# The last product of a group of eight, issued as two halves of 256 columns

## The chip, the cores and the metric

One Trainium2 chip, of which the kernel uses one core. The metric is the device time of one execution in microseconds (us), and the kernel before has a median of 450.82 us over 3 runs.

## What is computed

Sliding-window attention with 32 global positions for 8 batches of 8 heads, then a mixture of 8 experts (hidden size 1024) on the 4352 rows of 512 values that the attention gives. A row takes part only where its skip score is positive, goes to one expert, and is replaced by itself plus the gated result.

```python
def _moe_ref(x, w_skip, w_gate, w1, w2):
    do_compute = x @ w_skip > 0
    out = x.copy()
    xc = x[do_compute]
    e_idx = np.argmax(xc @ w_gate, axis=1)      # gate_w: softmax of the logits at e_idx
    for e in range(E):
        mask = e_idx == e
        h = np.maximum(xc[mask] @ w1[e], 0.0)
        y[mask] = gate_w[mask, None] * (h @ w2[e])
    out[do_compute] = xc + y
    return out
```

## The kernel before

The first half of the program (to about 219 us) is the attention, with the routing of its rows to lists by expert. The change is in the second half, the expert stage. There the rows of an expert are gathered in tiles of 128, two tiles (256 rows) at a time. Weights and activations are split in a high and a low part, so that each product of fp32 accuracy is three matmuls: high by high, high by low, low by high. The eight experts run one after the other, and the weights, tokens and hidden tiles lie in two sets of buffers that alternate by expert.

`ffn` is the body of an expert. Line 933 makes the hidden values of both tiles: eight groups of 12 matmuls (128x256 each), one group for each 128 hidden units, every group into one of the four PSUM banks `sb`; ScalarE (line 939) and VectorE (line 940) turn each into the high and low parts `hh` and `hlw`. Then comes the first tile of results (`py0`, by `part(py0, 0, ...)`): eight product groups `f`, three matmuls of 512 columns each (line 950), and `put`, which scales by the gate, adds the row on VectorE (line 1047) and scatters it to the output from GpSimd (line 1051).

What follows depends on how many rows the expert has, read from a register at run time:

- few rows: `short`, a second tile of at most 64 rows, in two column halves of 256, two matmuls for each of eight groups (line 985), with its own VectorE operations (line 991);
- more rows: `full`, the whole second tile by `part(py, 1, ...)`, also at line 950. In the main body its last two product groups are held back and issued by `rest_of`, and its `put` (into `ylast`) comes at the end of the expert;
- over 256 rows: also a third tile, by `ffn_half` (the half body): hidden values with the operands the other way round (line 1012), transposes (line 1023), then eight product groups into `sb[3]` (line 1038) and `put`;
- still more rows: `beyond`, another `ffn` over the further rows of the list.

The order on each engine is the one in which the program is written (a manual schedule). In the program's order, line 933 of the next expert follows at once on TensorE behind the last matmul of line 985, of line 1038, or of `rest_of`. Transposes of the next expert's rows (line 211) are issued between the first and the second tile.

In the profiled execution, the main body of the experts 0 to 7 starts on TensorE at about 219, 265, 286, 307, 343, 364, 399 and 422 us. Expert 0 has a further list, whose line 933 starts at 243.76 us.

## Time and profile before

| | us |
|---|---|
| median of 3 runs | 450.82 (449.47 to 453.19) |
| the profiled execution, its own time | 450.12 |
| its span, first to last instruction | 448.2 |
| TensorE busy | 424.5 (95%) |
| TensorE weight loads busy (beside its matmuls) | 366.2 (82%) |
| VectorE, ScalarE, GpSimd busy | 308.3, 286.5, 223.3 |
| mean granted clock of TensorE | 0.992 of full speed |

The profile is of one execution. Times are counted from the first instruction; a row names the line, the engine, the operation, the tile written and the tiles read. PE is TensorE's matmul, PEld its weight load, DVE VectorE, ACT ScalarE, POOL GpSimd; a q behind an engine is its sequencer. Matmuls are pipelined: the start of one to the start of the next is what one costs, and its own duration is longer than that.

### The profile page before, as it was taken

What the parts mean: (1) busy time and instruction counts of PE and PEld (TensorE: products, weight loads), DVE (VectorE), ACT (ScalarE), POOL (GpSimd) and SP (SyncE); (2) the same over time, 40 slices, a digit from 0 to 9 for tenths busy, and PEclk for the clock granted to TensorE, in tenths of its full rate; (3) what the DMA queues carried; (4) which work ended last, traced back from release to release, by engine and by line L of the source; (5) the groups of instructions that cost most, each with busy time, mean ns of one, the idle gap of its engine ahead of it and who ended that gap; (6) DMA issues with size and microseconds to landing.
All of it is one profiled execution on the core that took longest, in us unless ns stands there. A gap on an engine that the chain in (4) does not pass through costs nothing.

```text
span 448.2 us, 13744 instructions
## 1 busy us (share of the span) xinstructions
PE 424.5 (95%) x5002; PEld 366.2 (82%) x5002; DVE 308.3 (69%) x1222; ACT 286.5 (64%) x872; POOL 223.3 (50%) x233
## 2 busy tenths in 40 slices
PE   7799999998989999978999999999999999999995
PEld 3587787877767877666997999999888999889894
DVE  6898787997878878986662249586724868249352
ACT  5599999999888998866451238375523745237240
POOL 7568677778985688887367114223101321013101
PEclk9699999999999999999999999999999999999999
DMA  7998999898999789531435607594910949209101
GB/s 255 314 317 271 312 322 315 278 326 279 287 261 322 231 239 288 161 120 49 81 134 118 247 31 271 193 316 161 346 74 9 314 181 353 106 22 319 72 4 34
DMA packets 50773, 93.35 MB, mean 208 GB/s; under 512 B 15820, under 2 KB 20172, under 8 KB 50672
## 3 DMA queue, kind: packets, MB, share of 16 engines
q1 hardware_dynamic: 44992, 79.73, 54.8%
q0 software_dynamic: 5680, 12.34, 8.7%
q8 instruction: 55, 0.90, 0.8%
q14 instruction: 46, 0.38, 0.3%
HBM read 81.07 MB, written 14.01 MB: 212 GB/s over the span
## 4 chain that ended last, share of the span: by engine, by line
DMA 43%; PE 19%; ACT 11%; issue 10%; DVE 8%; POOL 7%; SPq 1%; POOLq 1%; another core or an unknown queue 0%; ACTq 0%
DMA out_dram<-yo,six 18%; DMA xsecond<-out_dram,six 9%; ACT prob L403 8%; DMA xfirst<-out_dram,six 7%; DMA out_dram<-xr 4%; PE pv L544 4%; PE pss L385 3%; PE pst L481 3%; DVE prob L398 2%; DMA lst<-dat,slu 2%; POOL prob L440 2%; PE pr L602 2%; PE pv L556 1%; PE psg L449 1%; PE psgT L497 1%
## 5 line engine op out<-in xcount | busy, mean ns | idle before, releaser
L403 ACT ACTIVATE prob<-prob,nmx 128x160 f32<-128x160 f32 x256 | 106.8, 423 | 16.1 <-DVE nmx L398 15.3
L440 POOL TENSOR_TENSOR prob<-prob,inv 128x640 f32<-128x640 f32 x64 | 80.6, 1260 | 33.0 <-DVE inv L436 19.0
L1051 POOL DMA_INDIRECT out_dram<-yo,six x12 | 12.1, 1012 | 111.9 <-DVE yo L1047 108.6
L939 ACT ACTIVATE hh<-ph 128x256 fp32r<-128x256 f32 x72 | 27.7, 384 | 54.9 <-PE ph L933 47.3
L385 PE MATMUL pss<-ks,qs 64*64 64x160 f32 x1024 | 52.0, 309 | 1.8 <-DVE nmx L398 1.1
L403 ACT ACTIVATION_READ_ACCUMULATOR prob<-prob,nmx 128x1 f32 x256 | 49.6, 194 | 0.0
L544 PEld LDWEIGHTS pv<-ptT,vw 128*64 128x64 f32 x1024 | 41.4, 139 | 9.2 <-issue 8.6
L544 PE MATMUL pv<-ptT,vw 128*64 128x64 f32 (+1 forms) x1024 | 46.3, 238 | 0.0
L933 PE MATMUL ph<-xl,w1h 128*128 128x256 f32 x288 | 45.1, 279 | 0.2 <-DVE yo L991 0.2
L933 PE MATMUL ph<-xh,w1h 128*128 128x256 f32 x288 | 45.2, 279 | 0.0
L933 PE MATMUL ph<-xh,w1l 128*128 128x256 f32 x288 | 44.9, 278 | 0.0
L385 PEld LDWEIGHTS pss<-ks,qs 64*64 64x64 f32 x1024 | 35.1, 135 | 9.3 <-issue 5.3
L940 DVE SCALAR_TENSOR_TENSOR hlw<-ph,hh 128x256 fp32r<-128x256 f32 x72 | 30.1, 418 | 17.8 <-ACT hh L939 17.4
L693 POOL DMA_INDIRECT lst<-dat,slu x34 | 34.0, 1000 | 14.4 <-DVE cni L1080 5.8
L950 PE MATMUL py<-w2h,hh 128*128 128x512 f32 x104 | 41.1, 396 | 0.0
L950 PE MATMUL py<-w2h,hlw 128*128 128x512 f32 x104 | 40.6, 391 | 0.0
L950 PE MATMUL py<-w2l,hh 128*128 128x512 f32 x104 | 40.6, 390 | 0.0
L481 PE MATMUL pst<-ident,prob 128*128 128x128 f32 x256 | 39.7, 281 | 0.0
L933 PEld LDWEIGHTS ph<-xh,w1h 128*128 128x128 f32 x288 | 38.8, 188 | 0.3
L933 PEld LDWEIGHTS ph<-xl,w1h 128*128 128x128 f32 x288 | 38.5, 189 | 0.4 <-DVE yo L991 0.4
L933 PEld LDWEIGHTS ph<-xh,w1l 128*128 128x128 f32 x288 | 38.4, 188 | 0.0
L194 DVE TENSOR_TENSOR w2l<-raw,w2h 128x1024 fp32r<-128x1024 f32 x28 | 34.1, 1217 | 3.9 <-ACT w2h L193 3.9
(193 smaller groups left out, 990.3 us busy)
## 6 DMA issues: line engine op xcount, KB each, us to landing
raw<-in_w_dram SPq DMA_DIRECT2D x56, 512.0 KB, 6.2
vw<-in_v_dram SPq DMA_DIRECT2D x32, 512.0 KB, 6.4
ks<-in_kT_dram SPq DMA_DIRECT2D x32, 400.0 KB, 5.4
out_dram<-xr SPq DMA_DIRECT2D x32, 256.0 KB, 5.3
qs<-in_qT_dram SPq DMA_DIRECT2D x31, 256.0 KB, 4.9
raw<-in_w_dram POOLq DMA_DIRECT2D x8, 512.0 KB, 7.2
vgs<-in_vgl_dram SPq DMA_DIRECT2D x32, 64.0 KB, 6.4
lst<-dat,slu POOLq DMA_INDIRECT x34, 5.0
```

What stands on the lines that cost most here:

```text
L194: eng.tensor_sub(lo, raw, hi.bitcast(F32))
L385: nc.tensor.matmul(banks[odd][head(h ^ odd), j * W:(j + 1) * W], q[head(h), w * QB:(w + 1) * QB], window(k[head(h)], w), start=True, stop= ...
L403: nc.scalar.activation(pt[:, i, :], pt[:, i, :], AF.Exp, bias=nmx[:, i:i + 1], scale=-1.0, accum_out=sums[:, i, 0:1],)
L440: nc.gpsimd.tensor_mul(pt[:, sl, :], pt[:, sl, :], inv[:, sl].unsqueeze(2).to_broadcast([P, 4, W]),)
L481: nc.tensor.transpose(pst[:, i * P:(i + 1) * P], pt[:, 4 * hf + i, 0:KW], ident)
L544: nc.tensor.matmul(pv[head(h), j * 96:j * 96 + n], vv[:, w, head(h)], ptT[:, w, h ^ odd, 0:n], start=False, stop=j == 3, skip_group_check= ...
L693: ins = nc.gpsimd.indirect_dma_start(out=lst, out_offset=bass.IndirectOffsetOnAxis(ap=slu[:, t:t + 1], axis=0), in_=dat[:, bs[j], t - 4 * ...
L933: nc.tensor.matmul(ph[:, 0:GRP], hl[a][:, c, f * P:(f + 1) * P], bb[:, c, :], start=i == 0, stop=i == 3 * NC - 1,)
L939: nc.scalar.activation(hh[:, f, :], ph[:, 0:GRP], AF.Relu)
L940: nc.vector.scalar_tensor_tensor(hlw[:, f, :], ph[:, 0:GRP], 0.0, hh[:, f, :].bitcast(F32), ALU.max, ALU.subtract,)
L950: nc.tensor.matmul(py, a[:, f, t * P:(t + 1) * P], hl[bb][:, f, :], start=f == 0 and i == 0, stop=f == NF - 1 and i == 2,)
L1051: ins = nc.gpsimd.indirect_dma_start(out=out, out_offset=bass.IndirectOffsetOnAxis(ap=sidx, axis=0), in_=yo, in_offset=None, bounds_check= ...
```

## The change

In the second tile (`t` = 1) of `part` and in `ffn_half`, the last of the eight product groups is issued as two column halves: all three terms for the columns 0 to 255, then all three for 256 to 511, six matmuls of 256 columns where there were three of 512. The flag that closes the accumulation stands on the last of the six. The first seven groups, the first tiles, and `short` stay as they are, as do the operations that read the result.

```diff
     LAST = 2
+    WHOLE = [slice(0, DM)]
+
+    def tail(f):
+        return WHOLE if f < NF - 1 else [slice(c, c + 256) for c in range(0, DM, 256)]
+
@@ in ffn @@
         def part(py, t, fs):
             for f in fs:
-                for i, (a, bb) in enumerate(terms):
-                    nc.tensor.matmul(
-                        py, a[:, f, t * P:(t + 1) * P], hl[bb][:, f, :],
-                        start=f == 0 and i == 0, stop=f == NF - 1 and i == 2,
-                    )
+                for cs in tail(f) if t else WHOLE:
+                    for i, (a, bb) in enumerate(terms):
+                        nc.tensor.matmul(
+                            py[:, cs], a[:, f, t * P:(t + 1) * P], hl[bb][:, f, cs],
+                            start=f == 0 and i == 0, stop=f == NF - 1 and i == 2 and cs.stop == DM,
+                        )
@@ in ffn_half @@
-            for i, (a, bb) in enumerate(((hh, "w2h"), (hh, "w2l"), (hlw, "w2h"))):
-                nc.tensor.matmul(
-                    py, a[:, f, 0:P], hl[bb][:, f, :],
-                    start=f == 0 and i == 0, stop=f == NF - 1 and i == 2,
-                )
+            for cs in tail(f):
+                for i, (a, bb) in enumerate(((hh, "w2h"), (hh, "w2l"), (hlw, "w2h"))):
+                    nc.tensor.matmul(
+                        py[:, cs], a[:, f, 0:P], hl[bb][:, f, cs],
+                        start=f == 0 and i == 0, stop=f == NF - 1 and i == 2 and cs.stop == DM,
+                    )
```

## Rows read from the trace of the kernel before

**Rows 1.** The page: span, and busy time of TensorE (us, share, instructions).

```profile
span 448.2 us, 13744 instructions
PE 424.5 (95%) x5002; PEld 366.2 (82%) x5002; DVE 308.3 (69%) x1222; ACT 286.5 (64%) x872; POOL 223.3 (50%) x233
```

**Rows 2.** Busy us by stretch: length, PE, PEld, DVE, ACT, POOL; clock, DMA share, GB/s.

```profile
226.00:442.90 216.90, 216.11 (x1468) 198.02 (x1466) 123.85 (x184) 96.58 (x157) 55.47 (x54) 1.00 0.49 167
442.90:448.20 5.30, 0.00 (x0) 0.00 (x0) 0.96 (x2) 0.00 (x0) 0.91 (x1) 0.95 0.08 18
```

**Rows 3.** Waits of TensorE from 228 us on: us in total, times, longest.

```profile
PE xt L211 <- DMA xmore<-out_dram,six: 0.6, 1, 0.6
PE ph L933 <- DVE yo L991: 0.2, 1, 0.2
```

**Rows 4.** Instructions of lines 950 and 1047: count; ns min/median/max; first and last start.

```profile
L950 PE MATMUL py<-w2h,hlw x104: 388/389/398, 231.4 to 438.7; 128*128 128x512 f32 x104
...
L1047 DVE SCALAR_TENSOR_TENSOR ylast<-py,lt,xfirst x2: 750/750/751, 266.1 to 422.3; 128x512 f32<-128x512 f32 x2
L1047 DVE SCALAR_TENSOR_TENSOR yo<-ph,lt,xmore x2: 751/752/752, 342.8 to 399.3; 128x512 f32<-128x512 f32 x2
L1047 DVE SCALAR_TENSOR_TENSOR ylast<-py,lt,xsecond x2: 743/743/743, 343.4 to 400.0; 128x512 f32<-128x512 f32 x2
```

**Rows 5.** Timeline of TensorE in expert 7 (start, us, what): line 950, then 985.

```profile
437.99 0.39 PE L950 MATMUL py<-w2h,hlw 128*128 128x512 f32 x1
...
438.67 0.39 PE L950 MATMUL py<-w2h,hlw 128*128 128x512 f32 x1
438.89 0.28 PE L985 MATMUL py<-w2h,hh 128*128 128x256 f32 x1
...
439.61 0.28 PE L985 MATMUL py<-w2h,hh 128*128 128x256 f32 x1
```

**Rows 6.** The same of line 933 alone: length, PE, PEld; clock, DMA share, GB/s.

```profile
243.76:254.65 10.89, 10.89 (x96) 10.85 (x95) 1.00 0.87 316
286.37:297.27 10.90, 10.90 (x96) 10.86 (x96) 1.00 0.52 157
307.43:318.33 10.90, 10.90 (x96) 10.87 (x96) 1.00 0.50 149
342.51:353.82 11.31, 11.30 (x96) 11.26 (x95) 1.00 0.54 175
363.97:374.87 10.90, 10.90 (x96) 10.86 (x96) 1.00 0.52 163
399.04:410.35 11.31, 11.31 (x96) 11.26 (x95) 1.00 0.59 196
422.15:433.46 11.31, 11.31 (x96) 11.26 (x95) 1.00 0.07 26
```

**Rows 7.** Timeline of TensorE: what stands ahead of line 933 in four bodies.

```profile
243.53 0.40 PE L950 MATMUL py<-w2h,hlw 128*128 128x512 f32 x1
...
286.25 0.28 PE L985 MATMUL py<-w2l,hh 128*128 128x256 f32 x1
...
342.29 0.39 PE L1038 MATMUL ph<-w2h,hlw 128*128 128x512 f32 x1
...
421.92 0.39 PE L950 MATMUL py<-w2h,hlw 128*128 128x512 f32 x1
```

**Rows 8.** Timeline of TensorE's weight loads: end of expert 6, start of expert 7.

```profile
421.70 0.19 PEld L950 LDWEIGHTS py<-w2h,hlw 128*128 128x128 f32 x1
421.93 0.65 PEld L933 LDWEIGHTS ph<-xh,w1h 128*128 128x128 f32 x4
```

**Rows 9.** Timeline: VectorE's operation behind the half body of expert 3.

```profile
342.78 0.75 DVE L1047 SCALAR_TENSOR_TENSOR yo<-ph,lt,xmore 128x512 f32<-128x512 f32 x1 [2.83 <-PE ph L1038]
```

**Rows 10.** Branches of TensorE's sequencer (ns min/median/max; first and last start), end of expert 6.

```profile
L1189 PEldq COMPARE_BRANCH  x2: 83/1496/2909, 417.5 to 418.1; - x2
L1204 PEldq COMPARE_BRANCH  x1: 187/187/187, 421.0 to 421.0; - x1
```

## Prediction

> **What bounds the kernel now.** I read the page first: TensorE is busy 424.5 of 448.2 us [rows 1]. That is an average, so I then asked for the two stretches that matter to an edit in the expert stage. From 226 to 442.9 us TensorE is busy 216.11 of 216.90 us at a granted clock of 1.00, and in the 5.3 us that remain it does nothing: two DVE operations and one scatter end the kernel [rows 2]. The waits of TensorE in that stage are one of 0.6 us for a gather and one of 0.2 us for a DVE result [rows 3]. So the reader is to see a stage in which every nanosecond that TensorE's stream of products grows or shrinks moves the end by the same amount, and in which no other engine has to be asked first. The chain of waits on the page gives 18% to the DMA out_dram<-yo; it is a long span between a scatter and something much later, and TensorE never stands still for it, so I set that view aside.

> **What runs of the changed lines.** Line 950 issues each of its three terms 104 times, that is 13 groups of eight [rows 4]. Nine are first tiles (eight experts and the one further list of expert 0), which the change leaves alone. Four are second tiles: their results are the four 128x512 `ylast` operations of line 1047, two from xfirst and two from xsecond [rows 4]. The two 128x512 operations `yo<-ph` belong to half bodies [rows 4]. So six products change, in experts 0, 3, 5 and 6 (second tiles) and 3 and 5 (half bodies). In each, three 128x512 matmuls become six 128x256 ones: 18 more matmuls and 18 more weight loads run, nothing else is issued, and no DMA, wait or buffer is added. The put still reads all 512 columns and so still waits for the very last matmul.

> **Step A, the products themselves.** Three 512-column matmuls take 0.68 us from start to start (437.99 to 438.67), and right behind them six 256-column ones over the same two operands, hh and w2, take 0.72 us (438.89 to 439.61) [rows 5]. Each product therefore grows by 0.04 us, six by 0.24 us. As a lower bound, the fast pace of line 933 below, 10.90/96 = 0.1135 us a matmul, gives 0.68 and a growth of nothing. I take 0.24, because line 985 has the same operands. [...]

> The 18 extra weight loads take 0.19 us each [rows 8], 3.4 us in all. They cost nothing beyond this pace, because a load starts right behind the start of the matmul ahead of it (the load at 421.93, the matmul at 421.92 [rows 7, 8]) and is done while that one streams. If that cover went, 3.4 us would be the bill.

> **Step B, what comes behind them.** This is where I expect the larger term. Line 933 is the same 96 matmuls of 128x256 in every expert, yet it takes two different times [rows 6]: 10.89 or 10.90 us in four of the stretches shown, and 11.31 us in three. TensorE is busy throughout in both, the clock is 1.00 in both, and DMA does not sort them (a share of 0.87 in a short one, 0.07 in a long one). Nor do the buffers, which alternate by expert: experts 2 (at 286.37) and 4 (at 342.51) use the same ones and differ, and so do experts 3 (at 307.43) and 7 (at 422.15). What sorts them is what TensorE ran just before. Ahead of the 10.90 ones at 286.37, 307.43 and 363.97 stand the 256-column products of line 985 (the row at 286.25 is one of them); ahead of the 11.31 ones at 342.51, 399.04 and 422.15 stands a long run of 512-column products, line 1038 or line 950 (the rows at 342.29 and 421.92) [rows 7]. The stretch at 243.76 follows 512-column products too and is short; but there only six of them (two product groups, the last at 243.53 [rows 7]) stand behind the wait of 0.6 us for the gather [rows 3], which I read as too few to settle. So TensorE's stream seems to carry a phase over from one group to the next: a settled run of 512 columns hands on the slow one, 256-column products hand on the fast one, and line 933 keeps what it is handed for all 96.

> The change puts six 256-column products at exactly the three places ahead of a slow stretch. If six are enough to hand on the fast phase, three stretches save 0.41 us each, 1.23 us. That six are enough is a choice: behind 512 columns, line 985 goes from 438.89 to 439.61 at an even 0.12 us [rows 5], which is the pace that it holds for its 32. Against it: line 933 itself runs 96 matmuls of 256 columns in the slow phase without leaving it, so 256 columns alone is not the cure; the operands of w2 and hh may be.

> In expert 0 the changed product is followed by the stretch at 243.76, which is fast already, and in experts 3 and 5 the changed second tile by line 1012; I put nothing there. If the first lost its fast phase it would cost 0.41 us.

> **Step C, waits.** The put of a half body starts 0.1 us after the last matmul's end, at 342.78, and takes 0.75 us [rows 9]. Its bank is wanted again by the fourth of the eight groups of line 933, about 342.51 + 3 x 1.41 = 346.7 us, so a put that comes 0.04 us later is hidden by 3 us of other products. The put of a second tile is queued behind other DVE work and is no one's releaser on TensorE. The tail after 442.9 us is the short body of expert 7 and is not touched.

> **The sum.** +0.24 - 1.23 = -0.99 us. Against the profiled execution, 450.12 us (span 448.2), that is 449.13; against the median of the three runs, 450.82, it is 449.83. The four times known of the kernel lie from 449.47 to 453.19, and the middle of 450.12 and 450.82 is 450.47; from there the forecast is 449.5 us. A measurement of this kernel can tell about 1% from no change, 4.5 us, so this is no change.

> **The rivals.** *The phase doesn't flip.* Then step A stands alone: 450.47 + 0.24 = 450.7 us. For it speaks that line 933 never leaves the slow phase by itself; against it, the three fast stretches behind line 985. Chance 0.30.

> *The jump out of the expert's branch is no longer covered*, and the kernel is slower. At the end of expert 6 TensorE's sequencer spends 2.91 us in one compare-and-branch of line 1189 from 418.1, then 0.19 us in that of line 1204 from 421.0 [rows 10], while the engine works through the products queued ahead of it; the first load of the next expert starts at 421.93 [rows 8]. The margin is 421.93 - 421.19 = 0.7 us. The change lengthens the code of every expert, and the sequencer has six more instructions to pass ahead of that jump. A second stay of 2.91 us in that chain would leave 2.2 us of standing TensorE. Once, with step A, that is 452.9 us; at the ends of experts 3, 5 and 6 all three, 450.47 + 0.24 + 6.6 = 457.3 us. It decides from the point at which the second branch ends after 421.93. Against it: the two other branches there take 0.08 and 0.19 us [rows 10], and six more instructions come with 0.04 us more of products. [...] Chance 0.06 for one such place, 0.02 for all three.

> *Something makes it faster by over 1%.* Nothing in the stage is large enough: all seven stretches at the fast pace are worth 1.23 us. Chance 0.02.

> **How the numbers follow.** Flip 0.60 (449.5), no flip 0.30 (450.7), one uncovered jump 0.06 (452.9, within 1%), three 0.02 (457.3, slower), faster 0.02. The first three are all no change; for a median of three times that spread as those of before did I move 0.01 more to faster and 0.02 to slower, which gives faster 0.03, the same 0.93, slower 0.04. The range has to hold the first two cases and the spread of the runs: downward 449.47 - 0.99 = 448.5 and a little, upward 450.82 + 0.24 = 451.1 and some of the way to 453.19: 448.3 to 452.0 us.

> **What the changed profile would show.** Step A: lines 950 and 1038 with 36 matmuls of 128x256 in the place of 18 of 128x512, and 0.68 to 0.72 us from the first of six to the first of what follows. Step B right: the stretches of line 933 in experts 4, 6 and 7 at 10.90 instead of 11.31 us, their matmuls 276 ns instead of 281. Step B wrong: they stay at 11.31. Step C: no new waits of TensorE from 226 us on, and the put of a half body still 0.1 us behind its last matmul. The slower rival would show as idle TensorE ahead of the first load of line 933 in experts 4, 6 or 7. The prediction is wrong if TensorE stands still anywhere in the stage where it does not now, or if other pieces of its stream (lines 1012 and 950 behind the changed products) change pace by more than 0.2 us.

## The result

The changed kernel takes 455.37 us (median of 17 runs, 453.3 to 457.7), the kernel before 450.92 us (17 runs, 449.47 to 453.19): a ratio of 1.0091, with an interval of 1.0073 to 1.0109. It is slower by 0.9%, some 4.4 us. The forecast was 449.5 us in a range of 448.3 to 452.0, so it was wrong.

The page after, where TensorE is busy 2.5 us longer in a span that is 6.3 us longer (in [rows 1] 424.5 of 448.2):

```profile
span 454.5 us, 13779 instructions
PE 427.0 (94%) x5020; PEld 367.8 (81%) x5020; DVE 308.6 (68%) x1222; ACT 286.1 (63%) x872; POOL 223.4 (49%) x233
```

The 18 more matmuls are there (5020 instead of 5002). What is new is idle time. The waits of TensorE from 222 us on, beside which [rows 3] has only the last two (us in total, times, longest):

```profile
PE py L991 <- issue: 2.3, 1, 2.3
PE xt L211 <- issue: 1.3, 1, 1.3
PE xt L211 <- DMA xmore<-out_dram,six: 0.8, 1, 0.8
PE ph L938 <- DVE yo L997: 0.2, 1, 0.2
```

"issue" is a wait for nothing that the profile shows: no engine and no transfer releases it. So the next question is what TensorE's sequencer did. Line 991 is 985 of before, 938 is 933, 956 is 950 and 1045 is 1038. First its branches in the kernel before, at the same two places, expert 4's branch into the short body and expert 5's branch ahead of its half body (ns min/median/max; first and last start in us):

```profile
L1204 PEldq COMPARE_BRANCH  x1: 446/446/446, 355.9 to 355.9; - x1
L1186 PEldq COMPARE_BRANCH  x1: 2422/2422/2422, 381.6 to 381.6; - x1
```

and the same two in the changed kernel:

```profile
L1211 PEldq COMPARE_BRANCH  x1: 3033/3033/3033, 357.3 to 357.3; - x1
L1193 PEldq COMPARE_BRANCH  x1: 4605/4605/4605, 386.8 to 386.8; - x1
```

One branch takes 2.6 us longer, the other 2.2. The two waits stand differently to them. Expert 5's branch is no longer covered by the products queued ahead: it ends at 391.40 us, and behind the last of these products TensorE stands still for 1.3 us, up to the transposes of line 211:

```profile
390.30 0.39 PE L956 MATMUL py<-w2h,hlw 128*128 128x512 f32 x1
391.96 0.63 PE L211 MATMUL xt<-ident,xmore 128*128 128x128 f32 x4 [1.27 <-issue]
```

Expert 4's branch is still covered: TensorE works through it and is idle for 0.09 us behind it. The stop of 2.3 us comes 3 us after its end, inside the short body, behind 15 of its 32 matmuls, where nothing branches:

```profile
359.99 0.39 PE L956 MATMUL py<-w2h,hlw 128*128 128x512 f32 x1
360.47 1.07 PE L211 MATMUL xt<-ident,xsecond 128*128 128x128 f32 x8
361.29 0.36 PE L991 MATMUL py<-w2h,hh 128*128 128x256 f32 x1
...
363.04 0.28 PE L991 MATMUL py<-w2h,hh 128*128 128x256 f32 x1
365.63 0.28 PE L991 MATMUL py<-w2l,hh 128*128 128x256 f32 x1 [2.31 <-issue]
```

And line 938, the same seven bodies as in [rows 6] (length, PE, PEld; clock, DMA share, GB/s):

```profile
244.71:255.60 10.89, 10.89 (x96) 10.86 (x96) 1.00 0.89 316
287.66:298.56 10.90, 10.90 (x96) 10.87 (x96) 1.00 0.49 158
308.73:319.63 10.90, 10.90 (x96) 10.86 (x96) 1.00 0.50 159
343.86:354.76 10.90, 10.90 (x96) 10.87 (x96) 1.00 0.53 175
368.52:380.09 11.57, 11.57 (x96) 11.53 (x96) 0.94 0.51 157
405.76:416.66 10.90, 10.90 (x96) 10.87 (x96) 1.00 0.55 170
428.75:439.75 11.00, 11.00 (x96) 10.96 (x96) 1.00 0.07 26
```

The three stretches of 11.31 us are at 10.90, 10.90 and 11.00: what the change was forecast to give, it gives. But expert 5's, at 10.90 before, has a granted clock of 0.94 and takes 11.57. The stretch around it:

```profile
361.29:366.55 5.26, 2.95 (x26) 2.86 (x25) 1.85 (x4) 0.92 (x2) 1.02 (x1) 1.00 0.49 190
366.55:369.96 3.41, 3.41 (x18) 3.41 (x17) 1.36 (x3) 0.00 (x0) 0.00 (x0) 0.50 0.02 5
```

TensorE stood still for 2.3 us up to 365.63; from 366.55 to 369.96 its granted clock was 0.50, though it was busy all of that time. So more than the stop is lost here: the half clock begins 0.92 us after it ended.

The account, by the starts of line 938 in both profiles:

| from ... to | before | after | difference, us |
|---|---|---|---|
| start of the program to expert 0 (attention) | 219.13 | 219.79 | +0.66 |
| expert 0 to expert 4 | 123.38 | 124.07 | +0.69 |
| expert 4 to 5 | 21.46 | 24.66 | +3.20 |
| expert 5 to 6 | 35.07 | 37.24 | +2.17 |
| expert 6 to 7 | 23.11 | 22.99 | -0.12 |
| expert 7 to the last matmul's start | 20.46 | 20.17 | -0.29 |

Experts 4 and 5 make 5.4 of the 6.3 us of this pair of profiles, and they hold the two waits and the half clock. The pair is further apart than the medians: the profiled executions took 456.45 us, 1.1 above the median, and 450.12, 0.8 below it.

### The profile page after: what moved, and what is told of

Its sections match the earlier page's. It is cut to its first block, busy times and chain, and to the rows that moved or that the text cites. A ratio compares the mean times of both kernels' runs of the same rounds, so it can differ in the third digit from the quotient of the medians.

```text
span 454.5 us, 13779 instructions
## 1 busy us (share of the span) xinstructions
PE 427.0 (94%) x5020; PEld 367.8 (81%) x5020; DVE 308.6 (68%) x1222; ACT 286.1 (63%) x872; POOL 223.4 (49%) x233
## 4 chain that ended last, share of the span: by engine, by line
DMA 37%; PE 20%; issue 14%; ACT 11%; DVE 8%; POOL 7%; POOLq 1%; SPq 0%; another core or an unknown queue 0%; ACTq 0%
DMA out_dram<-yo,six 20%; ACT prob L403 8%; DMA xfirst<-out_dram,six 7%; DMA out_dram<-ylast,six 4%; PE pv L544 4%; PE pss L385 3%; PE pst L481 3%; DVE prob L398 2%; POOL prob L440 2%; DMA out_dram<-xr 2%; DMA lst<-dat,slu 2%; PE pr L602 2%; PE pv L556 1%; PE psg L449 1%; POOL lst L693 1%
## 5 line engine op out<-in xcount | busy, mean ns | idle before, releaser
L956 PE MATMUL py<-w2h,hh 128*128 128x512 f32 (+1 forms) x108 | 41.8, 387 | 0.0
L956 PE MATMUL py<-w2h,hlw 128*128 128x512 f32 (+1 forms) x108 | 41.3, 382 | 0.0
L956 PE MATMUL py<-w2l,hh 128*128 128x512 f32 (+1 forms) x108 | 41.2, 382 | 0.0
L218 ACT CAST xh<-xt 128x512 fp32r<-128x512 f32 (+1 forms) x20 | 10.0, 548 | 42.8 <-PE xt L211 42.7
```

The source lines that it names most:

```text
L218: nc.scalar.copy(xh[:, c:c + step, ts_], p3[:, c:c + step])
L956: nc.tensor.matmul(py[:, cs], a[:, f, t * P:(t + 1) * P], hl[bb][:, f, cs], start=f == 0 and i == 0, stop=f == NF - 1 and i == 2 and cs.st ...
```

## The experiments

Theory A, formed from these rows: the loss is not in the products but in where the code lies. The six new instructions stand in six places of each expert's code (the half body, and five times the second tile's end, which is written out for each way the expert can go), 36 instructions per expert, most of them never reached. They move every later branch and target of TensorE's code; that the length of a branch depends on this is my supposition, which the experiments try. Theory B: the loss belongs to what runs, the split products, which put more instructions ahead of a branch or leave it less time. In the experiments code is lengthened by matmuls in the body for rows beyond 512, which is there for every expert and which none reaches with these inputs:

```diff
-    def ffn(e, x2, xg, gate, sidx, hook=lambda i: None, bank=ps_t, between=lambda f: None):
+    def ffn(e, x2, xg, gate, sidx, hook=lambda i: None, bank=ps_t, between=lambda f: None, pad=0):
...
         py0 = bank("py")
+        for _ in range(pad):
+            nc.tensor.matmul(py0, hh[:, 0, 0:P], hl["w2h"][:, 0, :], start=True, stop=True)
...
-    e, turn_x(xmore, e % 2), xmore, lambda t: lt2[:, t, 1:2], s2,
+    e, turn_x(xmore, e % 2), xmore, lambda t: lt2[:, t, 1:2], s2, pad=N,
```

**The code without the change.** The kernel before with N = 18 (16 in expert 1).

> The kernel before, its products whole, with 18 matmuls more (16 in expert 1) in each expert's body for rows beyond 512, which no expert reaches with these inputs: nothing more runs, but the code of TensorE behind it lies where it lies in the changed kernel, to within 4 instructions. Theory A (the loss is the place of the code, whose targets TensorE's sequencer has to wait for): 454 to 456 us, with a branch of about 3 us ahead of the short body of expert 4, one of 4 to 5 us in expert 5, and line 933 at 11.31 us in experts 4, 6 and 7 as before. Theory B (the loss belongs to the split products that run: more instructions ahead of the branch, or less time left above it because TensorE is faster): 450.5 to 451.5 us, no new idle time of TensorE.

456.34 us beside 450.99, a ratio of 1.0124 (1.0081 to 1.0167). Not one instruction more runs, and the kernel is slower by as much as the changed one, or more. Its waits of TensorE, and in the second fence its branches at the two places (line numbers differ by a few from kernel to kernel):

```profile
PE py L987 <- issue: 2.1, 1, 2.1
PE xt L211 <- DMA xmore<-out_dram,six: 1.4, 1, 1.4
PE xt L211 <- issue: 0.6, 1, 0.6
```

```profile
L1206 PEldq COMPARE_BRANCH  x1: 3209/3209/3209, 358.5 to 358.5; - x1
...
L1188 PEldq COMPARE_BRANCH  x1: 3380/3380/3380, 386.5 to 386.5; - x1
```

The stop in the short body of expert 4 is back, at 2.1 us; line 933 is at 11.31 us in experts 4 and 6 and 11.39 in expert 7, as whole products leave it. Theory B is out: it had no new idle time here. Expert 5's branch is under the 4 to 5 us expected, and nothing waits behind it here. Of the 5.2 us by which this profile's span is longer than that of before, the two waits for issue are 2.7; the attention (0.7), the wait for the gather (0.9) and line 933 of expert 1 (11.72 instead of 11.36 us) make another 2.

**The change without the place.** The changed kernel with N = 110, so that an expert's code is 256 instructions longer than before.

> The changed kernel with 110 matmuls more in the same bodies that no expert reaches, so that with the 36 instructions of the change each expert's code is 256 instructions longer than before and every branch and target lies, modulo 256, within 3 instructions of its place in the kernel before. What runs is what runs in the changed kernel. Theory A, with blocks of 256 instructions as the unit: no new idle time of TensorE, line 938 at 10.90 us in experts 4, 6 and 7, and 449.5 to 450.1 us, about 1 us under the kernel before. Theory B: the time of the changed kernel, 454 to 456 us.

450.91 us beside 450.99, 1.0006 (0.9983 to 1.0028). Its waits, and then the branch into expert 4's short body:

```profile
PE xt L211 <- DMA xmore<-out_dram,six: 1.2, 1, 1.2
PE ph L938 <- DVE yo L999: 0.2, 1, 0.2
```

```profile
L1213 PEldq COMPARE_BRANCH  x1: 446/446/446, 356.6 to 356.6; - x1
```

No wait for issue, the branch at the 446 ns of before, to the nanosecond, and line 938 at 10.90, 10.90 and 10.89 us. So the whole loss is gone with more unreached code instead of less, which is what theory A says and nothing else here does. The gain of 1 us, though, does not show in the median.

**Which product hands on the short pace.** Half bodies split alone, then second tiles alone, with code filled up in the same way (N = 125 and 113):

```diff
-                for cs in tail(f) if t else WHOLE:      # in part; for the half bodies alone
+                for cs in WHOLE:
-            for cs in tail(f):                          # in ffn_half; for the second tiles alone
+            for cs in WHOLE:
```

> Only the half bodies are split, the second tiles are whole; code filled up so that branches and targets lie modulo 256 within 4 instructions of the kernel before. The phase that line 938 takes over: 10.90 us in experts 4 and 6, 11.31 in expert 7, and 2 x 0.41 - 2 x 0.04 = 0.74 us less than before (450.2 us) if theory A holds; if the second tile ahead of the half body is needed too, 11.31 us in all three.

450.73 us, 0.9994 (0.9972 to 1.0016). Line 938 in experts 4, 6 and 7:

```profile
344.44:355.34 10.90, 10.90 (x96) 10.87 (x96) 1.00 0.52 174
400.61:411.51 10.90, 10.90 (x96) 10.86 (x96) 1.00 0.53 175
423.68:434.69 11.01, 11.01 (x96) 10.98 (x96) 1.00 0.07 26
```

> Only the second tiles are split, the half bodies are whole; code filled up in the same way. Line 938: 11.31 us in experts 4 and 6, behind whole half bodies, and 10.90 in expert 7, behind the split second tile of expert 6. 0.41 - 4 x 0.04 = 0.25 us less than before, which is no change.

451.96 us, 1.0026 (1.0005 to 1.0047). The same three:

```profile
342.41:353.71 11.30, 11.30 (x96) 11.26 (x95) 1.00 0.51 169
398.95:410.26 11.31, 11.31 (x96) 11.26 (x95) 1.00 0.57 197
422.09:432.99 10.90, 10.90 (x96) 10.87 (x96) 1.00 0.07 25
```

The time of this second kernel was to be 0.25 us under that of before and is about 1 us over it; no wait in its profile explains that, and it stays open. Of the stretches five of the six come as expected: where no wait comes between, it is the product right ahead of line 938 that decides. The sixth, 11.01 behind the whole second tile of the first of these kernels, is a miss: there TensorE waited 0.2 us for issue ahead of line 938, and the short pace followed. That the gap ended the long pace fits, but wasn't tried by itself.

**Fewer copies.** The halves only in the copies of the second tile's end for up to 384 rows (the last two lines are in `beyond`):

```diff
-        def part(py, t, fs):
+        def part(py, t, fs, halves=False):
-                for cs in tail(f) if t else WHOLE:
+                for cs in tail(f) if halves else WHOLE:
-                lambda: part(py, 1, range(NF - kept, NF)),
+                lambda halves=True: part(py, 1, range(NF - kept, NF), halves),
...
-                rest_of()
+                rest_of(False)
```

> The halves only where line 938 or line 1018 follows in the code of up to 384 rows: the half bodies, and the second tile's held-back groups outside the body for more than 384 rows. Each expert's code grows by 18 instructions instead of 36, with nothing to fill up. All the split products but that of expert 0 run as in the changed kernel. Theory A: the code lies elsewhere, so the waits of the changed kernel at its places (3 us at the short body of expert 4) go or move; as no target of a short body that runs is near the end of a block as found there, no new idle time, line 938 at 10.90 us in experts 4, 6 and 7, 450 to 451 us. Theory B (the split products that run): 454 to 456 us.

449.77 us beside 450.63, 0.9985 (0.9971 to 1.0000). In this profile nothing waits for issue ahead of a short body; line 938 takes 10.90, 10.90 and 10.96 us.

**Once more, and moved.** The kernel of the second experiment again, and then with 32 and 72 matmuls more in expert 0's unreached body (N = 142 and 182 there, 110 elsewhere).

> The kernel of e2_halves_moved once more, with more rounds, to size what is left of the gain. From its first profile (expert stage from 244 us on 1.1 us shorter than before): 449.9 us, a ratio of 0.9976. If instead something that a single profile hides takes it back, a ratio of 1.000 and runs in two groups.

450.48 us, 0.9993 (0.9979 to 1.0008): neither of the two readings fits well, there is no gain of 0.24%, and the twelve runs, 449.02 to 451.09, are not in two groups. The profile has a wait of 0.7 us for issue that the first profile of this very kernel hadn't, behind expert 0's branch of line 1169 (the row of the second experiment, then of this one):

```profile
L1169 PEldq COMPARE_BRANCH  x1: 1737/1737/1737, 258.6 to 258.6; - x1
```

```profile
L1169 PEldq COMPARE_BRANCH  x1: 3850/3850/3850, 258.6 to 258.6; - x1
```

The same branch of the same code takes 1.74 us in one execution and 3.85 in another. No cover was lost between the two, as the kernel is the same and line 938 ahead of the branch takes 10.89 us in both. What differs is when a packet on the instruction queue q8 came: it started 1.0 us before the branch in the first and 1.3 us after the branch began in the second.

> As e6_halves_again, with 32 matmuls more in the part of expert 0 that is not reached, so that all code from expert 1 on lies 64 instructions further on. Theory A says that the time depends on this though nothing that runs does; the branches of expert 4 stay 110 instructions or more away from the place that they have in the changed kernel, so no wait there; 449.5 to 452 us, the difference to e6 being the branch at the end of expert 6 and the one ahead of the half body of expert 5.

450.74 us, 0.9998 (0.9981 to 1.0014). No wait at expert 4, as expected; expert 1's branch into its short body takes 2.93 us instead, covered by the products ahead (no wait of TensorE for issue in this profile).

> As before with 72 matmuls more in the part of expert 0 that is not reached: the branch into the short body of expert 4 lies, modulo 256, where it lies in the changed kernel, those of the other experts do not. Theory A: the branch of about 3 us and the idle time of about 2 us come back in expert 4 and nowhere else; 452.5 to 454 us. If the place modulo 256 is not what counts: no wait there, the time of e6.

Three of its four runs take 456.48, 457.12 and 458.70 us, the fourth 463.34, beside 450.63: the middle one of the three is 1.4% over, and the ratio is 1.0207 (1.0158 to 1.0256). It is the slowest of all against the kernel before, from 40 unreached matmuls more than the last one. Its waits for issue, and then two branches, those of expert 4 and of expert 3:

```profile
PE py L993 <- issue: 3.1, 2, 1.8
PE xt L211 <- issue: 2.1, 1, 2.1
```

```profile
L1213 PEldq COMPARE_BRANCH  x1: 2619/2619/2619, 361.3 to 361.3; - x1
...
L1195 PEldq COMPARE_BRANCH  x1: 3738/3738/3738, 327.5 to 327.5; - x1
```

The branch put in expert 4's place did come back, at 2.62 us, and with it a stop inside that short body, of 1.2 us. "Nowhere else" was wrong: expert 3's branch ahead of its half body is at 3.74 us, with the stop of 2.1 us among the transposes behind it, and the short body of expert 2 stops behind two of its matmuls for 1.85 us, after which TensorE has a clock of 0.52 from 305.4 to 308.8 us. What runs is the same here and in the two kernels before, at 457.12 us (that middle run) and 450.48 and 450.74, so the place decides, but I can't yet say ahead of a run which places are bad.

**What can be kept.** The fewer copies twice more, and a smaller edit: only the third term of the last group in two halves, 6 instructions per expert instead of 36 (the half body is edited in the same way).

```diff
-                for cs in tail(f) if halves else WHOLE:
-                    for i, (a, bb) in enumerate(terms):
+                for i, (a, bb) in enumerate(terms):
+                    for cs in tail(f) if halves and i == 2 else WHOLE:
```

> The kernel of e5_fewer_copies once more, with five rounds, as its interval touched 1: 449.8 us, a ratio of 0.9985, if the 1.1 us that its profile shows in line 938 less the longer products is a gain that lasts; 1.000 if it was a matter of the first runs.

0.9988 (0.9949 to 1.0027): no difference can be read. The kernel before takes 458.23 us here and spreads by 9 us; in the profiles of this run and the next three, expert 0 starts at 226 to 228 us instead of 218 to 221, so the longer time lies ahead of the expert stage. The profile has a wait that the first one of this very kernel hadn't:

```profile
PE py L991 <- issue: 0.5, 1, 0.5
```

It stands behind expert 0's branch ahead of its short body, 3.61 us long here and 0.47 there. So the fewer copies are not free of such waits either.

> As e9, but only the third of the three terms of the last group is issued in two halves, so that two 256-column matmuls stand behind a run of 512 columns instead of six, and each expert's code grows by 6 instructions. If two are enough to hand on the short pace: line 938 at 10.90 us in experts 4, 6 and 7, and a ratio of 0.997 to 0.9985. If the phase needs the three or more that line 985 takes until its pace is even: 11.31 us there, and a ratio of 1.000.

0.9970 (0.9931 to 1.0009). Two 256-column matmuls are enough; line 938 in experts 4, 6 and 7, and behind them that of expert 0's further list:

```profile
350.28:361.18 10.90, 10.90 (x96) 10.86 (x96) 1.00 0.52 168
406.70:417.60 10.90, 10.90 (x96) 10.86 (x96) 1.00 0.58 192
429.42:440.32 10.90, 10.90 (x96) 10.86 (x96) 1.00 0.08 28
...
250.15:261.45 11.30, 11.30 (x96) 11.25 (x96) 1.00 0.84 308
```

The last was 10.89 us in the kernel before. Its products ahead are whole in both; what is missing here is the wait for the gather ahead of them. That takes back 0.41 us, and so it does in the next run of this kernel.

> The kernel of e10_last_term once more, as the times of that call spread by 2% on either side: 1.2 us of line 938 saved and six matmuls more, 449.5 to 450 us beside 450.6 of before, a ratio of 0.9975, unless the wait for the branch ahead of the half body of expert 5 (3.4 us in its first profile, 2.4 before) takes some of it back.

0.9957 (0.9921 to 0.9994).

> The kernel of e5_fewer_copies a third time, beside e11 on one chip: a ratio of 0.9985, and not under that of e11.

0.9953 (0.9914 to 0.9993). The changed kernel was not run beside these versions; by their ratios to the kernel before, both are 1.0 to 1.4% under it. Against the kernel before, the last two comparisons say 0.4 to 0.5% less and the other three of the same two kernels (0.9985, 0.9988, 0.9970) 0.1 to 0.3%, with intervals that reach 1. A small gain is likely, and 1.1 us of line 938 would be 0.24%; its size is not shown, and which of the two is the better can't be told.

## Why the prediction was wrong

**Step A, the products, held.** The six of a half body, and what follows:

```profile
343.15 0.28 PE L1045 MATMUL ph<-w2h,hh 128*128 128x256 f32 x1
...
343.74 0.28 PE L1045 MATMUL ph<-w2h,hlw 128*128 128x256 f32 x1
343.86 0.40 PE L938 MATMUL ph<-xh,w1h 128*128 128x256 f32 x2
```

0.71 us for 0.68, a growth of 0.03 where 0.04 was taken. The extra weight loads stayed hidden: they take 0.19 us each, and the six matmuls still start 0.11 or 0.12 us apart.

**Step B, the phase, held,** and with less than was thought to be needed: two matmuls do it. Three stretches gave 0.41, 0.41 and 0.31 us (11.31 to 10.90, 10.90 and 11.00); the third starts behind a short wait, and its first matmul alone takes 0.22 us. One reading in it did not hold. The stretch at 243.76 was taken to be short because six 512-column products are too few to settle. In the two profiles of the smaller edit the same six stand ahead of it without the wait for the gather, and it takes 11.30 us. So six are enough for the long pace, and the short one there seems to go with a wait or gap ahead; that was not tried by itself.

**Step C is the step that failed.** It put the waits at nothing: "nothing else is issued" and "no wait is added" counted what runs. The edit also adds what never runs, and the first experiment shows that this alone costs some 5 us (0.8 to 1.7% by its interval; 2.7 us of it stand in its profile as waits for issue). In the profile of the changed kernel the term that stood at nothing is 2.3 and 1.3 us of idle TensorE, and 1.5 us for the half clock behind the first of them: expert 5's line 938 lost 0.67 us (11.57 against 10.90), the short body before it 0.85 (its 32 starts take 7.23 us instead of 3.91; 2.47 of the 3.32 are the gap from 363.04 to 365.63 less one step of 0.12).

I had a rival near this, the jump that is no longer covered, and gave it 0.08; four things in it were wrong. Its cause was put in six more instructions to pass, not in the place of the code. Its places were the ends of experts 3, 5 and 6, since I had read the branches of one window, 417 to 422 us; asked for over the whole stage, the same view would have shown expert 5's branch, 2.42 us long before the change, as a second one at the edge. At the end of expert 6, where it looked, TensorE now waits for less than 0.1 us. Its mechanism covers only the 1.3 us in expert 5: the larger stop is inside the short body, 3 us after the branch. And its price had only the stop, 2.2 us, not the half clock that follows it.

For the waits in these two places the profile names no releaser; what it has ahead of them is packets on q8, a queue that it lists as "instruction". In the fourteen profiles, 52 branches of TensorE's sequencer from 222 us on take over 1 us, and each of them ends 1.30 to 1.67 us after a packet of 16 KB on q8 has landed (1.36 to 1.65 for the nine in the profiles of before and after). And from 14 to 218 us, where its sequencer has no branch, q8 of the kernel before brings 27 such packets while TensorE starts 6881 instructions (6735 matmuls and weight loads, 146 of its sequencer), 255 to a packet. The profile does not say whose queue q8 is; the even delay and this count are what tie it to TensorE, and that TensorE waits there for code that has not come yet is my reading of them. The branch of 3.03 us has its packet from 357.70 to 358.64 us. The stop in the short body ends in the same way: its packet comes from 363.02 to 364.05, and the next matmul starts 1.58 us later. The stops in the short bodies of the first experiment and of N = 182 (2.1, 1.85 and 1.2 us) end 1.21 to 1.34 us after theirs. The queue between 357.2 and 358.8 us, and between 362.9 and 364.1 (packets, MB, share of 16 engines):

```profile
q8 instruction: 1, 0.02, 3.7%
...
q8 instruction: 1, 0.02, 5.4%
```

The expectations count places in blocks of 256 instructions. The trace has 255 to a packet; that bad places repeat at this distance is not shown. With 256 instructions more per expert the loss was gone; with N = 182 the place counted on was bad again, with a branch of 2.62 us, and two that were not counted on were bad too, with a branch of 3.74 us in expert 3 and a stop of 1.85 us in expert 2. So the same products were slower or not as the code happened to fall, and which of the places are bad the runs do not say.

Why the sound versions gain less than the 1 us of the sum is shown in part. The branch at the end of expert 0 (1.74 or 3.85 us in one kernel, 0.47 or 3.61 in another) lies at the edge of its cover, differs from execution to execution, and left 0.3 to 0.7 us of idle TensorE in three of their ten profiles. Line 938 takes 11.72 instead of 11.35 us in expert 1 in three of the ten, and 11.30 in expert 0's further list in two.

## What to carry to other kernels

In this kernel, which branches at run time, code that never runs was not free: 18 such matmuls per expert (16 in one) cost 0.8 to 1.7%. So count the instructions that an edit adds to every copy, and look at the length of each branch of the sequencer and at what covers it, over the whole stage, and at the packets of the instruction queue ahead of every wait for issue. A slower result behind an edit that "does nothing" is tested by giving the old kernel the new kernel's code length, and the new one the old one's places. And where one loop of equal matmuls takes two times, look at what TensorE ran just ahead of it, and whether it waited there.
